# First batch's residual by a transposed DMA copy and VectorE adds, a new order of the first jobs, and two last stores on GpSimd's queue

## The chip, the cores and the metric

The kernel runs on one core of a Trainium2 chip. The metric is the device time of one execution in microseconds (us). A core has five engines with instruction streams of their own: TensorE (PE; its weight loads are listed as PEld), VectorE (DVE), ScalarE (ACT), GpSimd (POOL) and SyncE (SP). They meet through semaphores. SP, ACT and POOL also issue DMAs, which 16 DMA engines carry out. Matrix products land in PSUM, which the kernel uses as 8 banks of 128 x 512 fp32. Everything else lies in SBUF, 128 partitions wide.

## What is computed

Random-feature attention (8 batches, 8 heads, 576 tokens, 64 channels, 128 features), and an MLP mixer over its result, per batch 576 tokens x 512 channels:

```python
def phi(x):                      # x scaled by D ** -0.25
    h = x @ omega.T - (x * x).sum(-1, keepdims=True) / 2
    return exp(h - h.max(-1, keepdims=True)) / sqrt(m)
kv, z = phi(k).T @ v, phi(k).sum(tokens)
x = (phi(q) @ kv) / (phi(q) @ z + 1e-6)      # heads side by side: 576 x 512
u = x + (relu(x.T @ w_tok1) @ w_tok2).T      # token mix, 256 hidden
out = u + relu(u @ w_ch1) @ w_ch2            # channel mix, 1536 hidden
```

Inputs and outputs are fp32; inside, the products run in fp16.

## The kernel before

**Tiles.** Each batch has 512 main tokens (four tiles j of 128) and 64 tail tokens. Tails of two batches share 128 partitions, and all tails are channel-mixed at the end as a ninth "batch" c = 8.

**Stages of a batch.** `attention` makes the features kp and qp, per pair of heads (hp): a product on TensorE, an exponential on ScalarE (L499), for keys a maximum `km` and its reciprocal on VectorE (L652, L654), the scaled values `vs`, the kv product (L673, L680), its copy (L284), the numerator (L706) and the division (L715, L716). The tail tokens' keys go through L534 and `kt_max` (L573 to L576). `token_mix` has two hidden tiles (t1, L749), four output tiles (t2, L762), four VectorE adds that make u = x + h (`uadd`, L765), and on SP a DMA transpose u -> uT (`ut_dma`, L770), since the channel mix needs u with channels on partitions. `channel_mix` has twelve hidden tiles (c1, L938, four 128x512 products each, and a relu into r3) and then its output. For batches 1 to 8 that output is `channel_out_fast`: products of prepared sums (L888) and VectorE additions that read u and the bank (L877).

**Batch 0 is different.** `token_mix_first` makes uT straight from TensorE; u itself is never made. Its channel output is the plain one: for each of four tiles j, twelve products over the hidden tiles (L972) in three parts, and before the last of them four 128x128 products of uT with an identity (L970), which transpose u back into the PSUM bank and add it there as the residual. `out_copy` (L977, through L284) then copies the bank to o, twice on ACT (j = 0 and 2) and twice on DVE (j = 1 and 3), and a store (L982) issues from SP.

**Loads.** Batches 0 and 1 are loaded as they lie and transposed on TensorE. From batch 2 on, GpSimd's DMAs cast q and k to fp16 into a scratch in DRAM (`load_transposed`: k's tail L368, k's main part L362, q L357) and SP brings them back with DMA transposes (L378) as kT and qT. Those, and batch 2's above all, are spoken of below. Values come by GpSimd's DMAs too (L335, tails vt L349).

**What sets the order.** Every piece of work is a job with an engine and a cost, numbered as it is created. `run` (L136) executes the jobs in the order of a list written out by hand, `ORDER` (L22). So each engine issues its own jobs in that order, and a job that waits holds all later ones of its engine. A negative number in `ORDER` is a warm-up product of zeros on a bank. `SLOT` (L83) says which buffer of a ring each job takes (8 banks; three each of u, uT, kT, qT; two each of o and r3). `MOVED` (L93) and `BY` (L20) move single jobs between DVE, ACT, POOL and SP. A bank is given back by the job that reads it last, and the next user on TensorE waits for that reader.

**The last stores.** The tails' outputs leave in twelve small stores at the end of `channel_out_fast` (L911 to L919, issued at L917): six shapes, each once from SP and once from ACT. `need` names which quarter of the result they wait for.

Of the kernel before, what the change touches and what calls it, by code (L numbers as in the profile page):

```python
# [12 lines left out]
ALU = mybir.AluOpType  # L13
# [9 lines left out]
    6, 5, 0, 2, 3, 1, 4, 17, 15, 19, 7, 10, 13, -1, -2, -3, -4, -5, -6, -7, 49, 12, 40, 47, 8, 41, 43, 42, 48,  # L23
    23, 44, 50, -8, 45, 11, 108, 9, 123, 110, 51, 52, 22, 125, 46, -1, -4, 71, 124, 79, 14, 53, 72, 109, 32, 93,
    81, 57, 54, 95, 18, 55, 114, 58, 80, 30, 76, 67, 77, 20, 56, 74, -7, -7, -7, 96, 85, 73, 82, 75, 94, 97, -4,
    111, 68, 83, 99, 126, 112, 98, 21, -2, -2, 199, 78, 129, 86, -3, 63, 128, 84, 100, -8, 87, 201, 64, 88, 16,
    115, -6, -1, 101, 91, 89, 102, 235, 92, 200, 130, 103, 113, 65, 104, 237, 90, 59, 24, 236, 106, 66, 116,
    105, 27, 137, 117, 107, 25, 252, 127, 131, 60, 33, 253, 118, 120, 132, 141, 121, 26, 122, 133, 61, 142, 119,
    31, 135, 143, 138, 254, 136, 34, 249, 134, 238, 250, 145, 202, 240, 149, 251, 139, 144, 150, 35, 146, 151,
    62, 140, 332, 241, 239, 147, 329, 152, 203, 69, 221, 148, 255, 207, 224, 209, 153, 225, 154, 28, 70, 161,  # L30
    226, 256, 222, 159, 208, 223, 156, 162, 227, 157, 204, 210, 206, 177, 211, 155, 228, 169, 212, 213, 160,
    167, 333, 205, 173, 214, 257, 175, 242, 258, 178, 163, 158, 29, 176, 328, 261, 259, 164, 229, 174, 215, 165,
    230, 216, 262, 233, 243, 171, 244, 334, 166, 247, 36, 217, 172, 184, 327, 170, 168, 219, 189, 220, 234, 231,
    179, 232, 245, 180, 248, 331, 246, 190, 218, 181, 260, 191, 182, 263, 264, 266, 265, 194, 267, 183, 192,
    268, 330, 272, 269, 274, 273, 270, 275, 335, 271, 385, 337, 185, 336, 276, 387, 338, 343, 386, 371, 345,
    357, 391, 186, 339, 344, 358, 193, 373, 461, 195, 187, 359, 392, 37, 372, 346, 340, 374, 348, 462, 196, 377,
    375, 347, 277, 376, 197, 463, 360, 341, 388, 378, 363, 393, 362, 299, 394, 390, 283, 364, 379, 284, 289,
    380, 300, 278, 361, 291, 464, 342, 365, 38, 292, 287, 366, 389, 285, 288, 349, 383, 367, 286, 293, 465, 290,
    281, 294, 384, 350, 368, 369, 395, 295, 467, 396, 188, 397, 370, 198, 602, 381, 351, 297, 382, 598, 352,
    398, 355, 353, 298, 279, 356, 296, 603, 354, 282, 301, 468, 280, 39, 480, 399, 481, 303, 474, 466, 402, 304,  # L40
    302, 597, 305, 476, 400, 307, 403, 308, 311, 482, 401, 475, 309, 494, 310, 505, 496, 491, 306, 404, 507,
    312, 410, 495, 408, 411, 506, 315, 492, 405, 493, 409, 406, 316, 508, 469, 407, 519, 318, 521, 412, 470,
    471, 520, 522, 319, 510, 477, 313, 478, 511, 600, 523, 509, 317, 512, 323, 320, 599, 472, 321, 525, 473,
    435, 322, 526, 421, 497, 513, 422, 413, 524, 314, 479, 527, 498, 423, 436, 514, 325, 528, 414, 483, 601,
    415, 529, 499, 416, 530, 515, 427, 484, 500, 516, 531, 503, 731, 431, 428, 604, 532, 517, 417, 518, 736,
    501, 737, 419, 418, 502, 432, 733, 324, 485, 424, 433, 732, 486, 420, 504, 487, 425, 434, 488, 489, 429,
    426, 490, 630, 430, 533, 610, 534, 437, 612, 438, 611, 536, 441, 632, 442, 445, 535, 443, 537, 444, 631,
    439, 540, 446, 644, 655, 541, 544, 656, 542, 440, 646, 538, 326, 543, 449, 657, 545, 645, 539, 547, 450,
    546, 658, 627, 661, 660, 641, 452, 642, 628, 548, 629, 735, 447, 643, 659, 453, 613, 647, 605, 616, 607,
    457, 618, 734, 606, 614, 633, 648, 451, 617, 615, 608, 557, 634, 569, 609, 558, 619, 553, 649, 561, 554,  # L50
    620, 458, 565, 1006, 549, 566, 869, 650, 562, 635, 662, 559, 550, 636, 448, 570, 868, 637, 663, 560, 567,
    664, 454, 651, 667, 460, 738, 653, 555, 668, 654, 867, 563, 652, 621, 564, 639, 551, 622, 556, 640, 623,
    638, 625, 552, 665, 571, 666, 455, 626, 572, 624, 747, 573, 775, 748, 669, 574, 670, 568, 575, 749, 577,
    672, 777, 578, 776, 456, 581, 671, 579, 459, 673, 580, 871, 739, 750, 576, 741, 761, 674, 752, 582, 751,
    678, 675, 676, 740, 763, 679, 585, 762, 742, 680, 677, 587, 681, 586, 682, 789, 767, 764, 778, 588, 780,
    765, 766, 870, 768, 583, 589, 779, 790, 781, 743, 791, 593, 873, 590, 1003, 875, 792, 584, 877, 769, 1008,
    793, 591, 753, 794, 782, 876, 744, 594, 925, 872, 745, 697, 592, 754, 878, 691, 698, 1001, 927, 695, 770,
    874, 926, 795, 596, 687, 1002, 746, 755, 696, 783, 688, 773, 701, 774, 756, 796, 784, 759, 757, 699, 760,
    758, 771, 787, 700, 785, 692, 797, 689, 798, 772, 801, 705, 690, 802, 879, 786, 703, 706, 702, 799, 693,
    704, 788, 683, 800, 685, 684, 711, 694, 928, 686, 803, 911, 804, 707, 712, 806, 713, 805, 708, 715, 709,  # L60
    807, 710, 595, 714, 912, 810, 716, 930, 812, 929, 811, 814, 913, 808, 813, 719, 815, 809, 817, 720, 816,
    914, 818, 880, 883, 916, 722, 882, 881, 917, 1005, 721, 884, 915, 723, 885, 918, 886, 900, 724, 888, 897,
    727, 889, 1007, 899, 898, 725, 931, 890, 919, 819, 728, 920, 932, 887, 903, 730, 902, 891, 831, 1004, 901,
    892, 933, 726, 904, 825, 934, 832, 923, 833, 924, 1137, 841, 834, 893, 895, 842, 837, 894, 826, 820, 829,
    838, 921, 905, 823, 906, 896, 907, 937, 824, 835, 908, 909, 821, 836, 910, 922, 935, 839, 822, 938, 827,
    840, 936, 717, 828, 847, 830, 1017, 843, 1014, 939, 1019, 940, 848, 1018, 844, 1015, 942, 718, 1016, 849,
    851, 943, 845, 941, 729, 1034, 852, 1009, 1048, 1011, 944, 846, 1010, 1035, 948, 850, 946, 1049, 945, 950,
    1050, 947, 855, 1036, 949, 951, 1059, 1062, 856, 952, 1061, 1031, 857, 1023, 1032, 1064, 1060, 858, 1033,
    1138, 1065, 1063, 853, 859, 1066, 860, 1020, 1045, 1012, 1022, 863, 1046, 1021, 1037, 1013, 861, 1047, 854,
    1038, 973, 1051, 963, 1024, 953, 1052, 1067, 967, 1068, 964, 954, 1053, 1025, 974, 1054, 959, 862, 864,  # L70
    1069, 1071, 965, 1072, 866, 1139, 1026, 1057, 1039, 966, 1027, 971, 968, 1028, 865, 1055, 1029, 960, 972,
    961, 1040, 1070, 1041, 1043, 1030, 955, 1058, 969, 956, 1042, 957, 1056, 970, 962, 1044, 975, 958, 1073,
    977, 976, 1074, 978, 981, 1076, 982, 1075, 983, 985, 1077, 984, 979, 1078, 986, 1084, 980, 1080, 1079, 1087,
    1082, 1081, 989, 1085, 1088, 987, 990, 1140, 991, 1083, 1086, 992, 1145, 993, 994, 1147, 1146, 997, 995,
    1161, 1093, 1162, 1105, 1097, 1106, 998, 1103, 1111, 1104, 996, 1107, 1112, 1148, 1089, 1108, 1109, 1090,
    1098, 1101, 1110, 1095, 1094, 988, 1099, 1096, 999, 1091, 1100, 1102, 1153, 1117, 1092, 1118, 1000, 1163,
    1113, 1119, 1121, 1114, 1149, 1122, 1115, 1155, 1154, 1125, 1120, 1156, 1141, 1126, 1143, 1128, 1144, 1159,
    1129, 1142, 1127, 1151, 1130, 1116, 1133, 1152, 1150, 1131, 1134, 1136, 1157, 1164, 1165, 1160, 1132, 1123,
    1158, 1166, 1169, 1173, 1170, 1167, 1177, 1174, 1175, 1171, 1124, 1185, 1176, 1135, 1181, 1168, 1172, 1183,
    1182, 1179, 1178, 1184, 1187, 1180, 1201, 1190, 1188, 1189, 1202, 1186, 1191, 1197, 1192, 1204, 1195, 1198,  # L80
    1210, 1209, 1199, 1196, 1203, 1193, 1207, 1200, 1208, 1212, 1194, 1211, 1206, 1205,
]
SLOT = (  # L83
    "0010234056072110300612204735102705162011013422653131321705100372251101422307112015460726045331020410"
    "1506202741312504300161723463752131214023015013220136735207215100243726004310360721402263142010307312"
    "6003504115201051431722105643100171246710022430561270106332415101306132514322031125042111020036010231"
# [33 lines left out]
class Planner:  # L120
# [41 lines left out]
    def engine(self, usual):  # L162

        return MOVED.get(len(self.jobs), usual)
# [3 lines left out]
def kernel(  # L168
# [758 lines left out]
    def channel_mix(c, key, jt):  # L927
# [30 lines left out]
        if fast:  # L958
            channel_out_fast(c, key, jr)
            return  # L960
# [85 lines left out]
```

## Time and profile before

| what | value |
| --- | --- |
| time, median of 3 runs (lowest to highest) | 279.51 us (279.39 to 279.87) |
| the profiled execution: its time, its span | 279.96 us, 278.2 us |
| granted TensorE clock | 0.998 |
| 0 to 20 us: busy PE / DVE / ACT / POOL | 16.36 / 12.73 / 12.71 / 17.75 |
| 20 to 48 us | 28.00 / 22.02 / 18.13 / 18.57 |
| 48 to 57 us | 8.66 / 4.03 / 3.15 / 0.00 |
| 57 to 72 us | 14.63 / 12.81 / 12.54 / 7.62 |
| 72 to 85 us | 12.92 / 12.59 / 8.68 / 6.00 |
| 85 to 262 us | 177.00 / 146.22 / 80.60 / 42.60 |

The profile is of one execution. Its span runs from the first instruction to the last; the execution's time is that of the device around it. Busy times are of instructions that compute; DMA-issuing ones (SPq, ACTq, POOLq) are listed in the timeline but not counted. In a timeline row stand the start, the duration, the engine, the line of code, the operation, output <- inputs with their tiles, and in brackets how long the engine had been idle and what ended that. Rows of one line that follow each other are joined (x4). The chain that ended last is followed back from the last instruction, at each step to what released it.

### The profile page before, as it was taken

How to read it: one execution, taken by the hardware profiler on the slowest of the kernel's cores; microseconds unless marked ns; L12 is line 12 of the kernel's file. 1: busy time of each engine (PE TensorE's matmuls, PEld its weight loads, DVE VectorE, ACT ScalarE, POOL GpSimd, SP SyncE). 2: the span in 40 equal slices, each digit the busy share in tenths (PEclk: the TensorE clock that was granted, in tenths of full speed). 3: DMA queues.
4: the chain of work that ended last, by engine and by line, in shares of the span. 5: the costliest groups of instructions: out<-in, count | busy, mean ns of one | idle time of the engine just before them, and what ended most of it. 6: DMA issues, size and time to landing. Idle time of an engine off the chain costs nothing.

```text
span 278.2 us, 6130 instructions
## 1 busy us (share of the span) xinstructions
PE 268.6 (97%) x2459; PEld 167.2 (60%) x2459; DVE 220.2 (79%) x462; ACT 136.9 (49%) x284; POOL 92.5 (33%) x115
## 2 busy tenths in 40 slices
PE   7799999999999999999999999999999999999992
PEld 3458555444557655756676657655676477456781
DVE  3779678397996999987999799969995991595892
ACT  2788942397585337625756546635745500211200
POOL 8896782063722480076019600600052000000000
PEclk9999999999999999999999999999999999999999
DMA  7999999999996999979999987750342204030134
GB/s 192 173 201 197 206 209 157 183 211 170 202 204 136 188 180 179 189 138 156 202 182 191 236 104 113 179 123 0 103 71 84 88 10 87 0 153 0 75 105 125
DMA packets 84204, 39.66 MB, mean 143 GB/s; under 512 B 64208, under 2 KB 80784, under 8 KB 83984
## 3 DMA queue, kind: packets, MB, share of 16 engines
q0 software_dynamic: 34368, 17.48, 44.8%
q1 hardware_dynamic: 47504, 16.16, 29.2%
q10 hardware_dynamic: 2304, 5.64, 5.2%
q8 instruction: 19, 0.31, 0.4%
q14 instruction: 9, 0.07, 0.1%
HBM read 35.95 MB, written 16.52 MB: 189 GB/s over the span
## 4 chain that ended last, share of the span: by engine, by line
PE 75%; DMA 9%; DVE 6%; POOL 5%; issue 2%; ACT 1%; DVEq 0%; POOLq 0%; SPq 0%
PE bank L938 27%; PE bank L888 26%; PE bank L762 3%; PE bank L749 3%; DMA kT<-k 3%; PE bank L628 2%; PE bank L673 2%; DMA r<-in_q_dram 2%; DMA k<-in_k_dram 2%; PE bank L706 2%; PE bank L640 2%; DVE km L652 2%; POOL vs L293 2%; DMA vt<-in_v_dram 1%; DVE T L448 1%
## 5 line engine op out<-in xcount | busy, mean ns | idle before, releaser
L938 PE MATMUL bank<-uT,wc 128*128 128x512 f16 x376 | 89.5, 379 | 0.0
L288 ACT ACTIVATE r<-bank 128x512 f16<-128x512 f32 (+1 forms) x86 | 48.2, 600 | 78.9 <-PE bank L938 68.1
L293 POOL TENSOR_TENSOR vs<-v,vs 128x512 f16<-128x512 f16 x32 | 33.6, 1059 | 92.7 <-DVE vs L654 60.9
L938 PEld LDWEIGHTS <-wc 128*128 128x128 f16 x424 | 38.8, 98 | 37.3 <-issue 0.3
L888 PEld LDWEIGHTS <-r 128*128 128x128 f16 x384 | 36.9, 98 | 8.1 <-issue 0.7
L499 ACT ACTIVATE qp<-bank 128x512 f16<-128x512 f32 x64 | 36.7, 619 | 10.1 <-PE bank L640 7.3
L652 DVE TENSOR_REDUCE km<-kp 128x8 f16<-128x1024 f16 x32 | 38.7, 1208 | 2.6 <-ACT kp L499 2.4
L499 ACT ACTIVATE kp<-bank 128x512 f16<-128x512 f32 x64 | 35.7, 615 | 6.7 <-PE bank L628 5.5
L290 DVE TENSOR_SCALAR r<-bank 128x512 f16<-128x512 f32 (+1 forms) x40 | 26.1, 670 | 7.8 <-PE bank L938 6.8
L716 DVE TENSOR_TENSOR x<-bank,rc 128x320 f16<-128x320 f32 x62 | 30.5, 492 | 2.1
L888 PEld LDWEIGHTS <-S 128*128 128x128 f16 x288 | 28.0, 98 | 5.6 <-issue 0.4
L877 DVE TENSOR_TENSOR o<-u,bank 128x512 f32<-128x512 f16 x28 | 19.0, 679 | 7.8 <-PE bank L888 7.7
L888 PE MATMUL bank<-T,r 128*128 128x256 f16 x192 | 23.8, 273 | 0.0
L888 PE MATMUL bank<-T,S 128*128 128x256 f16 x192 | 23.6, 273 | 0.1
L888 PE MATMUL bank<-wc,r 128*128 128x256 f16 x192 | 23.4, 273 | 0.0
L765 DVE TENSOR_TENSOR u<-x,bank 128x512 f16<-128x512 f16 x28 | 17.7, 680 | 4.7 <-PE bank L762 4.7
L877 DVE TENSOR_TENSOR o<-o,bank 128x512 f32<-128x512 f32 (+1 forms) x27 | 16.5, 615 | 3.0 <-PE bank L888 2.6
L706 PEld LDWEIGHTS <-qp 128*128 128x128 f16 x256 | 13.8, 98 | 7.9 <-DVE kvsb L284 0.2
L715 DVE RECIPROCAL rc<-bank 128x5 f32<-128x5 f32 x62 | 11.5, 185 | 5.2 <-PE bank L708 3.9
L706 PE MATMUL bank<-kvsb,qp 128*128 128x65 f16 x256 | 15.5, 193 | 0.0
L673 PEld LDWEIGHTS <-kp 128*128 128x128 f16 x256 | 11.0, 98 | 5.5 <-issue 1.2
L762 PE MATMUL bank<-r,w 128*128 128x512 f16 x56 | 14.1, 381 | 0.0
(116 smaller groups left out, 364.9 us busy)
## 6 DMA issues: line engine op xcount, KB each, us to landing
out_dram<-o ACTq DMA_DIRECT2D x9, 512.0 KB, 3.2
q<-in_q_dram POOLq DMA_DIRECT2D x6, 576.0 KB, 9.2
wc<-in_moe_w_ch_dram POOLq DMA_DIRECT2D x4, 768.0 KB, 13.3
k<-in_k_dram POOLq DMA_DIRECT2D x6, 512.0 KB, 8.1
v<-in_v_dram POOLq DMA_DIRECT2D x6, 512.0 KB, 9.7
out_dram<-o SPq DMA_DIRECT2D x5, 512.0 KB, 3.3
r<-in_q_dram POOLq DMA_DIRECT2D x4, 256.0 KB, 7.9
v<-in_v_dram POOLq DMA_DIRECT2D x4, 256.0 KB, 8.2
```

The source lines that it names most:

```text
L288: nc.scalar.activation(out=out, in_=in_, func=AF.Relu)
L290: nc.vector.tensor_relu(out=out, in_=in_)
L293: (nc.gpsimd if eng == "POOL" else nc.vector).tensor_tensor(**kw)
L499: nc.scalar.activation(out=out, in_=in_, func=AF.Exp, bias=0.0, scale=1.0)
L652: nc.vector.reduce_max(out=mx, in_=kpv, axis=AX.X)
L706: nc.tensor.matmul(ps[:, k, j * 65 : (j + 1) * 65], st, s[:, i, 0 : D + 1], start=True, stop=True)
L716: nc.vector.tensor_tensor(out=t_x[place("x", b)][:, :, (2 * hp + hs[0]) * D : (2 * hp + hs[0] + n) * D].rearrange("p j (i d) -> p i j d", ...
L762: nc.tensor.matmul(ps, w2_of(tb, j), r1[:, tb, :], start=(tb == 0), stop=(tb == NT - 1))
L765: nc.vector.tensor_tensor(out=t_u[place("u", b)][:, j, :], in0=t_x[place("x", b)][:, j, :], in1=bank(n), op=ALU.add)
L877: nc.vector.tensor_tensor(out=o, in0=a, in1=ps, op=ALU.add)
L888: nc.tensor.matmul(ps[:, j * DH : (j + 1) * DH], a[:, cb, j * P : (j + 1) * P], w[:, cb, :], start=(bank_of(b, j0) not in held and j == j0 ...
L938: nc.tensor.matmul(ps, wc1[:, db, cb * P : (cb + 1) * P], moving(db), start=(db == 0), stop=(db == ND - 1))
```

## The change

Three things at once.

1. *Batch 0's residual.* The sixteen identity products leave TensorE. A new job `u_back` on SP transposes uT into a buffer of the u ring by DMA. The four copies from the bank become VectorE additions of u and bank, all on DVE, which wait for `u_back`.
2. *The order.* `ORDER`, `SLOT` and `MOVED` are new for the jobs of the first two batches, with a few swaps of neighbours later. The new job shifts all later numbers by one. `u_back` stands in SP's order right behind the back-transpose of batch 2's keys and ahead of that of its queries; uT of batch 1 follows. In GpSimd's order q's cast of batch 2 now stands ahead of the main part of k's. Warm-up products go from 20 to 25. Twelve jobs of ACT are on DVE after it (two of them the copies above), eleven of DVE on ACT, one of POOL on DVE, and two of batch 0's loads issue from ACT instead of SP.
3. *The last stores.* The two that need quarter "22" (128 KB each, one on SP and one on ACT before) issue from GpSimd.

In the file after, lines behind `ORDER` stand one later or one earlier than before: L378 is L379, `u_back` is L963, the additions are L977, the stores L981, the tail stores L918.

```diff
+        def u_back():
+            nc.sync.dma_start_transpose(out=t_u[place("u", c)].rearrange("p j (a c) -> p (j a) c", a=ND), in_=t_uT[place("uT", c)].rearrange("p j a c -> p (j a c)"))
+        j_u = dma("SP", key + 0.3, 2.6, u_back, deps=jt, take=[("u", c)], give=[("uT", c)], cost=3.5)
...
                     for cb in range(4 * part, 4 * part + 4):
-                        if cb == NCB - 1:
-                            for db in range(ND):
-                                nc.tensor.matmul(ps[:, db * P : (db + 1) * P], t_uT[place("uT", c)][:, j, db, :], ident16,
-                                                 start=False, stop=False, skip_group_check=True)
                         nc.tensor.matmul(ps, r3[:, cb, j * P : (j + 1) * P], wc2[:, cb, :], start=(cb == 0), stop=(cb == NCB - 1))
...
-            def out_copy(j=j, n=n, e_out=e_out):
-                copy(e_out, t_o[place("o", (c, j // 2))][:, j % 2], bank(n))
-            jo = add(e_out, 0.69, k2, out_copy, deps=[prev], take=[("o", (c, j // 2))], give=[("bank", n)])
+            def out_add(j=j, n=n):
+                nc.vector.tensor_tensor(out=t_o[place("o", (c, j // 2))][:, j % 2], in0=t_u[place("u", c)][:, j, :], in1=bank(n), op=ALU.add)
+            jo = add("DVE", 0.69, k2, out_add, deps=[prev, j_u], take=[("o", (c, j // 2))], give=[("bank", n), ("u", c)])
...
-                    eng = engine("ACT" if h else "SP")
+                    eng = engine("POOL" if need == "22" else "ACT" if h else "SP")
```

Of `ORDER`, the stretch around batch 2's back-transposes. Jobs before: 331 is kT and 330 qT of batch 2, 181, 186, 191, 196 are the last parts of the four output products, 182, 187, 192, 197 the copies. Jobs after: 332 is kT, 179 `u_back`, 331 qT, and 183, 188, 193, 198 are the additions.

```diff
-    179, 232, 245, 180, 248, 331, 246, 190, 218, 181, 260, 191, 182, 263, 264, 266, 265, 194, 267, 183, 192,
-    268, 330, 272, 269, 274, 273, 270, 275, 335, 271, 385, 337, 185, 336, 276, 387, 338, 343, 386, 371, 345,
+    246, 171, 158, 247, 173, 172, 164, 264, 265, 36, 195, 178, 266, 190, 180, 267, 332, 181, 268, 271, 191, 272,
+    174, 269, 179, 273, 275, 274, 196, 276, 192, 270, 331, 182, 336, 344, 338, 185, 346, 277, 337, 183, 358,
```

## The prediction

> **What bounds the kernel now.** I read the busy times first, then the 40 slices, then the chain that ended last. 0.2% of the time, 0.56 us, is about what a measurement of this kernel can tell from no change.
>
> ```profile
> PE 268.6 (97%) x2459; PEld 167.2 (60%) x2459; DVE 220.2 (79%) x462; ACT 136.9 (49%) x284; POOL 92.5 (33%) x115
> ...
> PE   7799999999999999999999999999999999999992
> ...
> PE 75%; DMA 9%; DVE 6%; POOL 5%; issue 2%; ACT 1%; DVEq 0%; POOLq 0%; SPq 0%
> ```
>
> TensorE is busy 97% of the span and is short of work only in the first slices and the last. By the windows it has all 177.00 of 177 us from 85 to 262, and the changed order leaves that stretch nearly as it was. So the time is decided by when TensorE leaves the first two batches, and by the tail behind its last matmul. The chain's longest pieces before 85 us lead to one place, batch 2's keys:
>
> ```profile
> 40.84 6.61 DMA k<-in_k_dram
> ...
> 47.54 8.19 DMA kT<-k
> ```
>
> Here are the queues around it: SyncE (SP), TensorE, VectorE (DVE), each from its timeline.
>
> ```profile
> 47.54 6.15 SPq L378 DMA_TRANSPOSE kT<-k  x1
> ...
> 54.35 2.61 SPq L378 DMA_TRANSPOSE qT<-q  x1
> 57.06 2.06 SPq L770 DMA_TRANSPOSE uT<-u  x1
> ```
>
> ```profile
> 49.00 0.39 PE L970 MATMUL bank<-ident,uT 128*128 128x128 f16 x4
> ...
> 55.77 0.28 PE L534 MATMUL bank<-omT,kT 64*128 64x128 f16 x4 [0.34 <-DMA kT<-k]
> ```
>
> ```profile
> 56.79 0.69 DVE L573 TENSOR_REDUCE kmt<-kpt 128x4 f16<-128x512 f16 x1
> ...
> 59.40 0.69 DVE L284 COPY o<-bank 128x512 f32<-128x512 f32 x1
> ...
> 66.07 0.30 DVE L284 CAST kvsb<-bank 128x130 f16<-128x130 f32 x1 [1.15 <-PE bank L680]
> ...
> 69.02 0.69 DVE L290 TENSOR_SCALAR r<-bank 128x512 f16<-128x512 f32 x1 [0.38 <-ACT kvsb L284]
> ```
>
> A start, a duration, and in brackets the idle time before it with its releaser. SP's first row is an issue that takes 6.15 us because the transpose's packets start only at 51.0, when the GpSimd queue's casts (v landed at 50.73) have drained; it lands at 55.73, and TensorE had waited 0.34 for it. VectorE from 56.79 on idles 1.15 + 0.38 only, until 71.64.
>
> **The change, part by part.**
>
> *Identity matmuls go.* Four groups of four 128x128 matmuls; sixteen in 0.89 to 0.90 us of starts (56 ns each): **-0.90** of TensorE. Two groups lie ahead of the kT gate at 55.77, where TensorE waits anyway, so -0.45 of it buys a longer wait.
>
> *u_back comes.* A transpose of 512 KB, in SP's order right behind kT of batch 2 and ahead of qT of batch 2. Its nearest rows are uT<-u, the same size and pattern: issue 2.06 us. From the end of issue to landing the rows give 2.04 (kT, 53.69 to 55.73), 2.11 (qT, 56.96 to 59.07) and 2.98 (uT, 59.11 to 62.09).
> When does kT land? In the new GpSimd order q's cast of batch 2 (576 KB) stands ahead of k's, so k reaches its scratch later than 47.45. But kT's packets did not start then: they started when the whole queue was empty. Its casts are the same, and walking GpSimd's new order by the old landings I find it empty at 50.3 to 50.8 instead of 51.0; I take 0.6 off, kT's issue end at 53.1 and its landing at 55.1. (Bounds 54.0 and 56.5: without the hole that its packets show from 52 to 53.5, or with the whole slip of k.) u_back, issued next, then ends its issue at 53.1 + 2.06 = 55.15 and lands at U = 57.2 by the first two rows, 58.1 by the third. I take **U = 57.2**, whose rows are the direct neighbours. Behind it qT ends its issue 2.61 later, at 57.76, and lands at 59.8; uT at 59.8 and 62.8. Two stores that stood between them now stand behind. Their first readers on TensorE stood at 60.16 and 63.84: covered by 0.4 and 1.0; what exceeds that cover would be a wait of TensorE.
>
> The Trainium skill (VectorE: DVE Perf Modes, "The three transpose paths" and its rules) speaks against this edit: a 128x128 transpose takes 390 ns on TensorE and 1309 ns through the DMA, and TensorE is to be used where PSUM will do. By that figure, as an estimate, sixteen blocks one by one would take 20.9 us, u_back would land near 76 and the body would be some 19 us longer. The rows disagree, and I give it no chance: the sixteen blocks of uT landed 3.02 us behind qT.
>
> *The adds.* Four VectorE adds (0.60 us start to start: the copy of 59.40, behind which the next starts at 60.01) replace two copies on VectorE and two on ScalarE: VectorE **+1.20**. The first add stands in VectorE's order behind the four uadds and ahead of kt_max (L573), its vbd and all four km of batch 2. So u_back's wait holds them all, and TensorE too: the second bank of the last kp pair is the one that this add frees. TensorE would reach it at about 56.9 and goes on at U + 0.7 = 57.9: a stall of 1.0.
> VectorE's sum: from 56.79 to 71.64 are 14.85 us, less the idle 1.53, so 13.32 of work, plus 1.20: 14.52. Started at U + 0.1 it ends at U + 14.62. The place that was at 71.64 is shifted by U - 57.0: at 57.2, **+0.2**. The two idle gaps are used up, and the shift is kept: VectorE is without a gap from 69.0 to 85.4, TensorE waits for its add at 82.54, and from 85 on all of TensorE is dense. TensorE's own path (gate 0.6 earlier, the two identity groups behind it -0.45, the stall +1.0) comes to -0.05: VectorE's ends last, and the two do not add. Body: +0.2, by the bounds of U (56.0 to 58.5) -1.0 to +1.5.
>
> *New order, moved engines, five more warm-ups.* Ahead of 20 us TensorE has 16.36 of 20 and waits for loads; warm-ups fill such holes, 0. About as many jobs go from ScalarE to VectorE as back, VectorE has 12.73 of the first 20 us and 22.02 of the next 28: room. Walking the new order through the loads I come to the first channel product within 0.5 of where it was. An earlier one is lost at the kT gate; a later one has 0.34 + 0.45 = 0.8 of cover there. I take 0; uncovered, +0.5 at most.
>
> *Tail.*
>
> ```profile
> 268.88 6.07 SPq L917 DMA_DIRECT2D out_dram<-o  x7
> ...
> 270.85 3.40 ACTq L917 DMA_DIRECT2D out_dram<-o  x5
> ...
> 273.03 0.42 DVE L877 TENSOR_TENSOR o<-o,bank 128x256 f32<-128x256 f32 x1 [0.23 <-PE bank L888]
> ```
>
> VectorE ends at 273.45, but SP issues its seventh store only at 274.47, behind its sixth (to 273.93) and 0.46 of wait for an older store's completion; it lands at 276.88, ScalarE's last at 276.70, and the span ends 1.3 later. With one store less in each, the last pair can issue near 273.5 and lands, by 2.2 (SP, 273.40 to 275.59) to 3.0 from issue (ScalarE, 273.68 to 276.70), at 275.7 to 276.5. GpSimd's two have their data by 271.7 to 272.0; the nearest row, GpSimd's vt load of 72.29, landed 4.25 after its start: 276.0 to 276.3. The last landing of 276.88 thus moves by -0.4 to -0.9; I take **-0.5**, near the late rows. None is gained if GpSimd's land 0.6 later than that row.
>
> *Sum.* +0.2 - 0.5 = -0.3 on the profiled execution's 279.96 (span 278.2), so 279.7. That execution stands 0.45 above the median of 279.51; against the median: 279.2, and **279.3** with the uncertain head leaning late.
>
> **Rivals.**
> *A, the forecast:* 279.3 (own range 278.7 to 280.0), chance 0.40.
> *B, u_back early.* kT shares the DMA engines with the casts instead of waiting for them, or the hole at 52 is missed. Against it: not one packet of kT before 51.0 with casts in flight. For it: a transpose into an idle queue, the uT of 85.50, landed 4.55 after its start, kT 8.19. kT at 54.0, U = 56.0: -1.0 - 0.5 gives 278.0 to **278.2**. Chance 0.30. The Trainium skill (DMA: Bandwidth & Descriptors, "SWDGE vs HWDGE vs iDMA") says that GpSimd's and SP's DMAs feed different queues inside each DMA engine, which takes them in turn; by that rule kT would move from its issue on, and this rival is the forecast. The trace shows no such turn before 51.0.
> *C, slower: u_back is the new gate.* On SP behind kT, whose k is now behind q on GpSimd's queue. Full slip: q's cast landed 2.86 behind v (50.73, 53.59), so k lands at 50.3, kT at 56.4, U = 58.5. VectorE's first add, kt_max, the km behind it and TensorE's bank all wait: +1.5 - 0.5 = +1.0, **280.5**. It decides from U = 58.1 on (1.06 above 57.0 eats the tail and 0.56). For it: the 2.98 row. Against: the queue's end, not k, held kT. Chance 0.22.
> *D, the tail gives nothing* (GpSimd's stores land last): 279.5 + 0.2 = **279.7**, chance 0.08.
>
> **Chances.** Faster by over 0.2% (below 278.95): B and a quarter of A, 0.40. Slower (above 280.07): C, with a little of A and D, 0.24. Within: 0.36. The range takes in B and C: 278.0 to 280.6.
>
> **What would show it.** No L970 groups; u_back's landing between 56.5 and 57.7, and VectorE's first add right behind it; kt_max and TensorE waiting there for the add; the last landing near 276.4 less the body's shift. I am wrong if u_back lands outside 56 to 58.5, if TensorE gets holes ahead of 48 us, or if the dense part from 85 on shifts by another amount than the add did.

## The result, and the profile after

The changed kernel takes 287.18 us (median of 6 runs, 284.89 to 290.96), the kernel before 279.25 (6 runs, 278.93 to 279.87): ratio 1.026, 95% interval 1.0231 to 1.0289, so 6.5 to 8.1 us slower. (The ratio leaves out the run of 290.96, in which TensorE's granted clock was lower, 0.986.) The forecast was 279.3, the range ended at 280.6. The profiled execution took 287.64, with a span of 285.9, 7.7 above that of before.

The busy line and the 40 slices of TensorE from the page after:

```profile
PE 273.2 (96%) x2448; PEld 168.4 (59%) x2448; DVE 224.8 (79%) x464; ACT 136.8 (48%) x283; POOL 92.5 (32%) x116
...
PE   6999999969899999999999999999999999999992
```

TensorE has 11 recorded products fewer (sixteen identity products less, five warm-ups more) and is nevertheless busy 4.6 us longer: the same products took longer somewhere. The slices from 85 us on are as full as before. Laying each TensorE job's start beside its start in the trace before shows where the time came from: the first channel product 35.44 instead of 30.42, the kT gate 60.52 instead of 55.77 (+4.74), from 85 to 275 us nearly every product +7.24 to +7.28 (a few swapped neighbours aside), the last products +7.98, the end of the span +7.69. So nearly all of it is there when the first two batches are done, and the gate is 4.7 late before `u_back` has made TensorE wait. Some 4.0 of these are TensorE's own: without its waits for kT it would have been there at 59.41, before at 55.43.

SP's, TensorE's and VectorE's timelines around the gate, after:

```profile
54.64 3.69 SPq L379 DMA_TRANSPOSE kT<-k  x1
58.43 2.17 SPq L963 DMA_TRANSPOSE u<-uT  x1
60.65 2.59 SPq L379 DMA_TRANSPOSE qT<-q  x1
63.33 2.67 SPq L771 DMA_TRANSPOSE uT<-u  x1
```

```profile
60.52 0.29 PE L535 MATMUL bank<-omT,kT 64*128 64x128 f16 x4 [1.11 <-DMA kT<-k]
...
63.99 0.38 PE L629 MATMUL bank<-omT,kT 64*128 64x128 f16 x7 [1.61 <-DVE o L977]
```

```profile
63.24 0.69 DVE L977 TENSOR_TENSOR o<-u,bank 128x512 f32<-128x512 f16 x1 [4.94 <-DMA u<-uT]
63.85 0.68 DVE L574 TENSOR_REDUCE kmt<-kpt 128x4 f16<-128x512 f16 x1
```

kT is issued at 54.64 (before 47.54) and lands at 60.47; `u_back` follows and lands at 63.15; the first addition starts 0.09 later, after VectorE has been idle 4.94 for it, kt_max right behind it; and TensorE waits 1.61 for the bank that the addition frees. These are the waits that the prediction named, at the places that it named, some six us later. The waits are not the origin, though: TensorE and kT were both late ahead of them. The DMA view of 18 to 28 us, before and then after, shows GpSimd's queue (q0) in that stretch:

```profile
q0 software_dynamic: 3149, 1.96, 127.3%
```

```profile
q0 software_dynamic: 3034, 1.25, 108.2%
```

(Packets, MB, share.) Before, the queue carried 1.96 MB in these 10 us, after only 1.25: the loads stood in GpSimd's order behind its vector work (L294 at 16.81 and 20.04), which waited for VectorE. Batch 2's casts follow: k's main part is issued at 42.58 instead of 29.66 and lands at 54.54 instead of 45.65, v at 57.89 instead of 50.73; q, which was moved ahead, at 52.08 instead of 53.59.

### The profile page after: what moved, and what is told of

Read it like the earlier page. It is cut to its first block, busy times and chain, and to the rows that moved or that the text cites. A ratio compares the mean times of both kernels' runs of the same rounds, so it can differ in the third digit from the quotient of the medians.

```text
span 285.9 us, 6132 instructions
## 1 busy us (share of the span) xinstructions
PE 273.2 (96%) x2448; PEld 168.4 (59%) x2448; DVE 224.8 (79%) x464; ACT 136.8 (48%) x283; POOL 92.5 (32%) x116
## 4 chain that ended last, share of the span: by engine, by line
PE 75%; DVE 9%; DMA 8%; issue 2%; SPq 2%; ACT 2%; POOL 1%; DVEq 0%
PE bank L939 26%; PE bank L889 26%; DMA k<-in_k_dram 4%; PE bank L763 3%; PE bank L750 3%; PE bank L629 3%; DVE km L653 2%; PE bank L641 2%; PE bank L707 2%; PE bank L674 2%; DMA wc<-in_k_dram 2%; PE bank L473 2%; DMA u<-uT 2%; PE bank L1012 2%; SPq L379 1%
## 5 line engine op out<-in xcount | busy, mean ns | idle before, releaser
L294 POOL TENSOR_TENSOR vs<-v,vs 128x512 f16<-128x512 f16 x31 | 32.6, 1057 | 95.9 <-DVE vs L655 64.9
L500 ACT ACTIVATE kp<-bank 128x512 f16<-128x512 f32 x64 | 36.3, 612 | 17.8 <-PE bank L629 17.8
L291 DVE TENSOR_SCALAR r<-bank 128x512 f16<-128x512 f32 (+1 forms) x41 | 26.9, 671 | 8.1 <-PE bank L939 7.4
L918 POOL DMA_DIRECT2D out_dram<-o x2 | 1.3, 644 | 61.5 <-DVE o L878 61.5
L716 DVE RECIPROCAL rc<-bank 128x5 f32<-128x5 f32 x62 | 11.5, 185 | 5.4 <-PE bank L709 4.9
L629 PE MATMUL bank<-omT,kT 64*128 64x128 f16 x256 | 13.6, 228 | 1.7 <-DVE o L977 1.6
```

The source lines that it names most:

```text
L291: nc.vector.tensor_relu(out=out, in_=in_)
L294: (nc.gpsimd if eng == "POOL" else nc.vector).tensor_tensor(**kw)
L500: nc.scalar.activation(out=out, in_=in_, func=AF.Exp, bias=0.0, scale=1.0)
L629: nc.tensor.matmul(ps[e][:, c : c + M], m[half[e], r, :], omT[half[e]], start=True, stop=True)
```

## The experiments

These are the seventeen kernels, each timed beside the kernel before on the same chip. A diff of the order shows the part of the list that was edited. The numbers of a job differ by the presence of `u_back`: e2, e4, e8 and e15, which have it, use those of the kernel after (there `u_back`, of batch 0, is 179), all others those of before. A negative number is a warm-up.

| kernel | ratio to before (95%) |
| --- | --- |
| changed | 1.026 (1.0231 to 1.0289) |
| e1 order only | 1.0178 (1.0151 to 1.0205) |
| e2 residual only, behind kT | 1.022 (1.0202 to 1.0238) |
| e3 stores only | 0.9994 (0.9984 to 1.0003) |
| e4 changed, u_back ahead of kT | 1.0327 (1.028 to 1.0374) |
| e5 order, sixteen warm-ups out | 1.0217 (1.0187 to 1.0247) |
| e6 order, loads first | 1.0162 (1.0145 to 1.018) |
| e7 both | 1.022 (1.0193 to 1.0247) |
| e8 residual only, ahead of kT | 1.0311 (1.0263 to 1.0359) |
| e9 order, first product first | 1.0217 (1.0171 to 1.0263) |
| e10 new head, old rest | 1.0129 (1.01 to 1.0158) |
| e11 old head, new rest | 1.0421 (1.0384 to 1.0457) |
| e12 order, three more warm-ups | 1.0108 (1.0082 to 1.0134) |
| e13 e12, loads and product first | 1.0147 (1.0127 to 1.0168) |
| e14 before, three fewer warm-ups | 1.0019 (1.0005 to 1.0033) |
| e15 before, and the transfer alone | 1.0221 (1.0197 to 1.0244) |
| e16 e12, thirteen warm-ups out | 1.0148 (1.0124 to 1.0172) |
| e17 e12, seven out | 1.0138 (1.0086 to 1.019) |

Theory 1 after the result: the new order makes the head late, and `u_back` adds to it. Theory 2: the wait for `u_back` is the cost. The first four take the change apart.

**e1, the order alone.** The old residual and stores in the changed kernel:

```diff
-        j_u = dma("SP", key + 0.3, 2.6, u_back, ...)
+                                nc.tensor.matmul(ps[:, db * P : (db + 1) * P], t_uT[...], ident16, ...)
-                    eng = engine("POOL" if need == "22" else "ACT" if h else "SP")
+                    eng = engine("ACT" if h else "SP")
```

> This is the changed kernel with the old residual (sixteen identity products, four copies, all on VectorE) and the old stores: the new order alone. Theory 1 (the new order makes the head late: it empties GpSimd's queue of casts late, so kT of batch 2 lands near 60.5 instead of 55.73, and u_back only adds its own 2.5 behind it): kT of batch 2 lands at 60 to 61, time 4.5 to 5.5 above before, 283.8 to 284.8. Theory 2 (the order is neutral, the wait for u_back costs the time): kT at 55 to 56, time within 1 of before. Theory 3 (each part costs about a third): about 2.5 above before.

283.71 against 278.88: 1.0178, some 5.0 of the 7.3 us. kT landed at 59.60. Theory 1 holds for the order.

**e2, the residual alone**, in the order of before, `u_back` behind kT:

```diff
-    ... 331, 246,
+    ... 332, 179, 247,
```

> The kernel before with u_back and the VectorE additions alone, in its own old order and stores; u_back stands behind kT of batch 2 on SP. Theory 1: kT lands at 55.7 as before, u_back some 2.7 later at 58.4, and by the rule of the prediction (u_back's landing less 57.0) TensorE is 1.4 later from 85 us on: 280.4 to 281.0. Theory 2: the wait for u_back makes most of the loss, 284 or more. Rival to both: the 0.9 of TensorE that goes is kept, 278.4 to 279.0.

1.022, 6.1 us: far over theory 1's 1.4 although `u_back` landed at 56.33, 2.43 behind kT. TensorE's waits in e2, the longest first (total, times, longest):

```profile
PE bank L760 <- DVE o L974: 3.5, 1, 3.5
```

In the old order the four output tiles are finished between 49 and 62 us and their banks copied out at once; now a tile that is finished earlier holds its bank until `u_back` lands, and batch 1's token mix (L760) waits for a bank 3.5 us. And the wait costs twice. The windows of e2 (busy PE ... POOL, then the granted clock, DMA share, GB/s):

```profile
54.00:56.00 2.00, 0.00 (x0) 0.00 (x0) 0.00 (x0) 0.00 (x0) 0.00 (x0) 1.00 0.97 183
...
60.00:62.00 2.00, 2.00 (x18) 0.89 (x18) 1.93 (x5) 0.71 (x3) 0.78 (x1) 0.50 1.03 221
62.00:64.00 2.00, 2.00 (x19) 0.98 (x15) 0.45 (x2) 2.00 (x5) 1.98 (x4) 0.50 1.07 204
64.00:66.00 2.00, 2.00 (x10) 0.65 (x10) 1.39 (x2) 1.04 (x3) 2.00 (x3) 0.71 1.18 147
66.00:68.00 2.00, 2.00 (x16) 0.61 (x14) 1.90 (x4) 1.82 (x4) 0.27 (x2) 1.00 0.88 164
```

After the gap TensorE is granted half its clock (0.58 from 58, 0.50, 0.50, 0.71) for 6.8 us by the trace's clock records (58.34 to 65.16), and does half the work: about 3.4 us more. The Trainium skill (TensorE: Matmul & The Clock Gate, Part 1) says that an idle window of about 3.4 us puts TensorE to half rate and that it takes at least one busy window to release it. The gap of 3.5 agrees with the first; the release took 6.8 us here and in e8, and 3.4 in e4 and e15. In the changed kernel's profile, where the gaps were 1.11 and 1.61, the clock stayed at 1.00.

**e3, the stores alone.**

```diff
-                    eng = engine("ACT" if h else "SP")
+                    eng = engine("POOL" if need == "22" else "ACT" if h else "SP")
```

> The kernel before with the two stores on GpSimd's queue alone. In the changed kernel the last landing came 3.28 behind the last VectorE instruction, before 3.43, and the end 4.44 behind it, before 4.73: 0.15 to 0.3 faster, 278.9 to 279.1. The prediction's size was 0.5 faster, 278.75. Rival: GpSimd's stores land last, 0.2 or more slower.

0.9994: 0.2 faster to no change (+0.08 to -0.45 us). The 0.5 of the prediction was too much. GpSimd's two landed at 273.63 and 274.64, ahead of the last one, from ScalarE, at 276.09.

**e4, the changed kernel with `u_back` ahead of kT.**

```diff
-    ..., 152, ..., 332, ..., 179, ...
+    ..., 152, 179, ..., 332, ...
```

> The changed kernel with one job moved: u_back ahead of kT of batch 2 in SP's order, right behind the job that finishes uT (SP is idle there until kT). Theory 1: u_back lands before 45, kT still near 60.5; what u_back added behind the gate (7.27 late from 85 us on, 4.74 late at the gate) goes: 2 to 3 below the changed kernel, 284.2 to 285.2. Theory 2: most of the loss goes, 279 to 281. Rival: the additions were not what VectorE was late for, nothing changes, 286.5 to 287.5.

1.0327, worse than the changed kernel, against both theories and the rival. `u_back` was in flight from 34.04 to 50.24, kT landed at 62.06, TensorE waited 3.9 for it and fell to 0.50 from 62 to 64.

**e8, the same in the old order.**

```diff
+    ..., 148, 179, ...
-    ..., 332, 179, ...
+    ..., 332, ...
```

> The kernel before with u_back and the additions, u_back right behind the job that finishes uT, some 15 us ahead of kT, in the old order. In the changed kernel with u_back first it was in flight from 34.04 to 50.24 beside GpSimd's casts, and k's cast landed 1.35 later than without that. So: u_back lands near 46 to 48, the wait of 3.5 on TensorE and the slow clock behind it are gone, kT lands 0 to 1.5 later, the 0.9 of identity products goes: 278.0 to 280.0. Rival (a transpose among the casts costs as much as it moves, 512 KB at about 190 GB/s is 2.7 us): 281 to 282.

1.0311, against the expectation and its rival. kT landed at 59.20 instead of 55.73, TensorE waited 4.1, the clock fell to 0.50. Hidden time on an idle queue (SP had nothing to do there) was no hidden time for the DMA engines, as e15 shows.

**e15, the transfer alone**: before, complete, and besides it `u_back`, read by nobody.

```diff
+        j_u = dma("SP", key + 0.3, 2.6, u_back, deps=jt, take=[("u", c)], give=[("uT", c), ("u", c)], cost=3.5)
...
+    ..., 148, 179, ...
```

> The kernel before, complete with identity products and copies, and besides them the transposed copy of uT into u, behind the job that finishes uT, read by nobody: the price of the transfer by itself. With the additions in it (287.6) k's cast of batch 2 landed at 49.48 instead of 45.65 and kT at 59.20 instead of 55.73, TensorE waited 4.1 and then ran at half rate for some 6 us. Theory D (the DMA engines are full up to the gate, so 512 KB more come on top): the same, 285.5 to 288. Theory A (the additions' waits were it): 279 to 280.

1.0221, 6.2 us: theory D, the transfer itself is the cost, with nobody waiting for it, because it shares the DMA engines with the casts. SP's timeline, the queues of 37 to 45 us, and TensorE's longest wait in e15:

```profile
29.94 8.26 SPq L960 DMA_TRANSPOSE u<-uT  x1
50.59 6.40 SPq L376 DMA_TRANSPOSE kT<-k  x1
```

```profile
q0 software_dynamic: 1285, 1.25, 92.7%
q1 hardware_dynamic: 1283, 0.33, 30.6%
```

```profile
PE bank L532 <- DMA kT<-k: 4.0, 1, 4.0
```

Two queues have work, and in eight us 1285 packets of the one and 1283 of the other are carried: they take turns, packet by packet. A packet of the transpose is 0.33 MB / 1283 = 0.26 KB, of a cast 0.97 KB. So 512 KB of transpose are about 2000 turns, last 20.1 us from issue to landing (30 to 50), and their time is taken from the casts that lead to kT, which lands at 59.05. The Trainium skill (DMA: Bandwidth & Descriptors, "Queues, rings and completion order") says that each DMA engine goes round the queues that have work, packet by packet; this trace agrees to two packets in 1285.

How dear was it? k's cast landed 3.1 us later than before (48.72 for 45.65). At the 197 GB/s that the view gives for this stretch 512 KB are 2.7 us, so the casts lost about what the transfer moved, the size that e8's rival had. The rest of the 6.2 us comes behind the gate: TensorE's wait of 4.0 brought 3.4 us of half clock with it, and in this profile TensorE also waited 1.8 for uT. e8 is 2.5 us slower still; what its additions cost there was not tried.

The other runs look for what makes the new order's head late; all have the old residual and stores, as e1.

**e5, fewer warm-ups, e6, loads first, e7, both.** e5 drops all warm-ups behind the ninth; e6 moves the DMA issues of batch 1's q, wc1, wc2, w1m and batch 2's k main cast ahead of GpSimd's vector work (e6's edit, GpSimd's jobs alone):

```diff
-    ... 75, ..., 27, ..., 115, 30, 86, 18, 32, 130, 25, 31, 333, 24, 29, 21, 26, 33, 332, 203, 28, 34, 35 ...
+    ... 75, ..., 27, 30, 18, 32, 21, 115, 86, 25, 24, 26, 130, 29, 33, 31, 34, 35, 333, 332, 329, 203, 28 ...
```

> The new order alone (old residual, old stores; 283.7 before this run) with nine of its 25 warm-up products: the sixteen that stand behind the first nine are out. Theory W (the thirteen of them between 15.06 and 19.09 stand in TensorE's way and cost their 3.1 us): the products behind them start 2 to 3 earlier, 281 to 282, if GpSimd's queue follows; where only the gate of batch 2's kT is left, 283.0. Theory P (GpSimd's order is what makes the gate late) and the prediction's zero (they fill holes): 283.4 to 284.0.

> The new order alone with GpSimd's DMA issues moved ahead of GpSimd's vector work that waits for VectorE: the loads of batch 1's q, of wc1 and wc2 and the cast of batch 2's k stand as early as in the order before. Theory P (the queue ran dry from 17 to 28 us because the issues stood behind that work, 242, 333, 148, 279 and 219 KB per 2 us where before had some 380): it stays full, kT of batch 2 lands at 55 to 57, time 280.0 to 281.5 unless TensorE's own head is as late as the gate. Theory H (TensorE's head is late by itself, it waited only 0.5 for the gate): kT early, but time 283.0 to 283.7.

> Both edits on the new order alone: sixteen warm-ups out and GpSimd's issues first. If both theories hold half (TensorE's head and the gate are late by about the same, so each alone hides the other's gain): 279.5 to 281, clearly below each alone. If P alone holds: as the run with the loads first. If the cause is elsewhere (order of TensorE's jobs, the first loads): above 282.5.

e6 did what it should: q0 stayed full (1.99 MB from 18 to 28 us), kT landed at 55.30, earlier than before. And the time is 1.0162, as e1 (1.0178) within the intervals. The first reader of kT on TensorE, in e6:

```profile
58.60 0.29 PE L533 MATMUL bank<-omT,kT 64*128 64x128 f16 x4
```

At 58.60 and with no wait: theory H, TensorE comes late by itself, the dry queue was not the bound. e6 changes one thing more: it issues k's cast ahead of q's, where the changed kernel has q first. GpSimd's timelines, after and then e6:

```profile
42.03 0.56 POOL L358 DMA_DIRECT2D q<-in_q_dram  x1
42.58 0.57 POOL L363 DMA_DIRECT2D k<-in_k_dram  x1
```

```profile
31.84 0.56 POOL L361 DMA_DIRECT2D k<-in_k_dram  x1 [2.60 <-DMA wc<-in_moe_w_ch_dram]
...
40.86 0.56 POOL L356 DMA_DIRECT2D q<-in_q_dram  x1
```

So the early kT is the work of both; the time did not follow either of them. e5 and e7 did not come out faster, and e7 is 1.6 us above e6: with sixteen warm-ups fewer the clock fell to half again (e7: from 18.2 to 25.1 us).

**e9, e10, e11.** e9 puts the first key product ahead of the third group of key transposes; e10 runs the new order's first 110 entries and then the old order; e11 the old order's first 120 and then the new.

```diff
-    ... 41, 49, 8, 47, 50, 9, 17, 45, 48, 14, 42, 46, 10, -6, -7, 108, 43, ...
+    ... 41, 42, 49, 8, 47, 50, 9, 17, 48, 108, 45, 14, 46, 10, -8, -1, 43, ...
```

> The new order alone, with its first key product (and the two VectorE copies that it needs) ahead of the third group of key transposes and of two warm-ups, which moved behind it to other banks. Theory H1 (ScalarE is what TensorE waits for up to 40 us; in the new order its first exponential starts at 9.84 instead of 7.59 us, and that is carried through): the first exponential starts near 8.3, 1.3 to 1.6 earlier, and the time falls by 1 to 1.6, to 282.2 to 282.8 (283.7 before). Theory H2 (the order behind 20 us is the cause): 283.4 to 284.0.

> The new order up to its 110th entry (TensorE at 20.2 us, all loads and warm-ups up to there), then the jobs that are left in the old order; old residual, old stores. In TensorE's ledger (time that is not useful products) the new order stands 1.0 to 1.6 above the old one at 20 us and 3.3 to 3.8 at 40 us. Theory H1 (the late start of ScalarE is carried through, the rest only shows it): most of the 4.8 stays, 282 to 283.8. Theory H2 (what follows 20 us is the cause): 280 to 281.

> The reverse: the old order up to its 120th entry (TensorE at 19.8 us), then the jobs that are left in the new order without its further warm-ups; old residual, old stores. Theory H1: 279.0 to 280.5. Theory H2: 282 to 284.

e9: the first exponential started at 8.37 instead of 9.84, but the next group of them came at 12.29 (12.76 in the changed kernel) and ScalarE idled 2.15 in between; nothing was gained. Theory H1 in this form (the late first product makes the head late) falls. e10: 1.0129, 3.6 of 5.0 us (2.8 to 4.4) come with what stands ahead of 20 us. e11 is inconclusive: the mixture had a wait of its own (TensorE 4.4 and 6.6 us for loads that the second order issues too late for the first).

**e12, three more warm-ups, and e14, three fewer in the old order.** The head's products, TensorE's timeline of before, after and e12:

```profile
4.40 1.06 PE L472 MATMUL bank<-S,wc 128*128 128x128 f32 x8
5.57 0.66 PE L472 MATMUL bank<-S,wc 128*128 128x128 f32 x4
```

```profile
4.92 1.94 PE L473 MATMUL bank<-S,wc 128*128 128x128 f32 x8 [1.16 <-DMA wc<-in_k_dram]
7.29 1.11 PE L473 MATMUL bank<-S,wc 128*128 128x128 f32 x4 [0.43 <-DMA wc<-in_k_dram]
```

```profile
4.83 1.14 PE L471 MATMUL bank<-S,wc 128*128 128x128 f32 x8
7.25 0.66 PE L471 MATMUL bank<-S,wc 128*128 128x128 f32 x4 [1.28 <-DMA wc<-in_k_dram]
```

The same eight products take 1.06 before and 1.94 after. The new order has five warm-ups and then a hole of 1.16, the old one seven without a hole. The clock column gives 1.00 in both stretches, but it counts time without a clock record as full. The kept traces' first record, to full clock, stands at 4.07 us before, at 13.41 after and at 5.02 in e12, and the durations change there: ahead of it the products run at half rate.

```diff
-    ... -1, -2, -3, -4, -5, 41, 49, ...
+    ... -1, -2, -3, -4, -5, 41, -6, -7, -8, 49, ...
```

> The new order alone with three more warm-up products in the hole of 1.2 us behind the first five (TensorE waits there for the first keys, 3.5 to 4.9 us). Theory C (in the new order that hole keeps TensorE at half rate up to 13.3 us: the same group of four key transposes takes 1.11 us against 0.66, eight key products 0.54 against 0.33, while the order before had seven warm-ups in a row and is at full rate from 4.4 us): the groups behind 5 us take 0.66 and 0.33, the head is 1 to 2 earlier at 20 us, time 281.5 to 282.7 (283.7 without). Theory L (the first loads decide when the head runs): rate up, time 283.3 to 284.0.

```diff
-    ... 13, -1, -2, -3, -4, -5, -6, -7, 49, ...
+    ... 13, -1, -2, -3, -4, 49, ...
```

> The kernel before with four instead of seven warm-up products at its start; nothing else. Theory C: the hole ahead of the first transposes holds TensorE at half rate for some us, the head loses 1 to 3, 280.2 to 282.2. Otherwise (they only fill a hole, the prediction's zero): 278.9 to 279.4.

e12 has the full rate from 5 us and 1.0108: 2.0 of the order's 5.0 us come back, with three products added. e14, whose first record stands at 8.08, loses 0.5 (0.1 to 0.9), less than expected: in its profile TensorE reaches the gate of batch 2's kT at 55.35, no later than before. Theory C, the cold rate, holds for two fifths of the order's loss.

**e13, e16, e17.** e13 adds e6's and e9's edits to e12; e16 takes the thirteen warm-ups at 12.61 and 15.12 us out of e12, e17 the first seven (shown).

```diff
-    ... 115, 112, -7, -7, -7, -7, -8, -8, -1, 53, ...
+    ... 115, 112, 53, ...
```

> The new order alone with the three warm-ups, the first key product first, and GpSimd's loads first. If the head's loss is the sum of cold clock, late first product and late loads, each hidden by the next: 279.5 to 281.5. If it lies in the order in which queries and keys of batch 0 come to ScalarE (idle 3.4 us longer up to 15 us): 282.5 to 283.7.

> The new order alone with the three early warm-ups (3.4 above before) and without the thirteen at 12.61 and 15.12 us. The first seven of these stand ahead of query transposes whose load landed at 12.35, the other six ahead of a query product. Theory W (at full rate they are in TensorE's way for up to 3.1 us): ScalarE gets its queries 1.5 to 3 earlier, 1 to 2.5 less, 0.9 to 2.4 above before. Theory Z (what stands behind them waits for copies and banks anyway): within 0.4 of the run with them, 3.0 to 3.8 above. Rival: the holes bring the half rate back, 5 or more above.

> The same with only the first seven out. Theory W: half of that gain, 0.6 to 1.5 less than with them, 1.9 to 2.8 above before; theory Z: 3.0 to 3.8 above.

None gained on e12. In e16 the granted clock was 0.88 up to 20 us and 0.75 to 24, in e17 0.91: whatever the warm-ups cost by standing ahead of the queries, they earned by keeping the rate. What makes the remaining 3.0 us of the new order stays open. If the 2.0 of the cold rate are part of e10's 3.6, about half of the 3.0 is set ahead of 20 us; neither GpSimd's loads, nor the first product, nor fewer warm-ups gave it back. e12 reaches the gate 1.6 us later than before and waits for nothing there; up to that place its eight warm-ups more than before take 1.65 us of TensorE. ScalarE, behind its first instruction and up to 15 us, is idle 8.4 us in the changed kernel and 6.2 in e12, against 4.7 before, but no run took that idle time away.

## Why the prediction was wrong

*The head.* "Walking the new order through the loads I come to the first channel product within 0.5 of where it was": it came 5.0 late (35.44 for 30.42). This is the step that failed. The term was put at 0, +0.5 at most, and e1 sizes it: 5.0 us. The prediction names no rate for the head, and the rate was half up to 13.4 us (11.5 in e1); e12 shows 2.0 of the 5.0 to come from that, and the cause of the other 3.0 stays open. Up to the gate both kernels do the same products, warm-ups and identity products aside. From start to start TensorE spends there 1.9 us more on the sixteen fp32 key transposes, 1.6 more on the key features, 1.0 on the five further warm-ups and 0.7 more idle; 0.6 less on the query features and 0.45 less on identity products. The cover of 0.8 at the gate was far too small for that.

*Warm-ups at 0.* Wrong in kind: they set the rate of what follows. Three more gave 2.0 back (e12), sixteen fewer took 1.6 us (e7 against e6).

*kT at 55.1.* It landed at 60.47. "I find it empty at 50.3 to 50.8": the queue was empty at 57.9, since its loads were issued late. Yet e6 shows that this was not the bound. The reading that kT's packets "started when the whole queue was empty" was wrong too: in the trace before the first came at 51.15, while q's cast landed only at 53.59, and e15's transpose shared the engines with the casts for 16 us. Behind its issue kT's first packet came 1.3 us (the changed kernel) to 4.2 us (e15) later. One thing holds in all nineteen traces: kT landed 1.8 to 3.4 us behind the last of batch 2's main casts, whichever that was, q in the old order (53.59, then 55.73) and v in the new one (57.89, then 60.47). The walk took v for the last one in the old order as well. Why kT follows the last cast is not shown.

*u_back at kT + 2.1.* It took 2.68 (60.47 to 63.15); in e2 2.43. Right in kind. The rule "U - 57.0" gives 6.15 for U = 63.15, the body was 7.27.

*What that wait is worth.* The forecast for `u_back` and the additions was +0.2. On top of the order's 1.0178 they make about 2.3 us of the changed kernel's 1.026. Alone, in the old order, they cost 6.1, and the order alone 5.0, together 7.3: the two do not add. Both make TensorE late around the same gate, which fits, but no run takes the overlap apart. The prediction had counted no gap long enough to lower the clock; in e2 and e8 the half clock cost about 3.4 us beside waits of 3.5 and 4.1, in e4 about 1.7 beside 3.9.

*Identity products, -0.90.* They went, and nothing of it could be seen in the time, as forecast.

*Tail, -0.5.* Mis-sized: alone 0.2 (e3), and no gain at all lies within the interval. In the changed kernel's profile one VectorE addition of the tail also waited 0.97 for a store of the ring to land.

*Rivals.* C ended on the right side, by the mechanism of `u_back` behind a late kT and with U beyond its 58.1; but its 280.5 was 6.7 too low, and its reason, k's cast behind q's, was never tried alone: e6 puts k ahead of q and fills the queue as well, and kT landed at 55.30. B's sharing of the engines is what the DMA engines do (e15), and it works against the kernel: the casts pay for it. The Trainium skill's rule of different queues taken in turn (DMA: Bandwidth & Descriptors, "SWDGE vs HWDGE vs iDMA"), which I set aside because no packet came before 51.0, was right about the sharing: e15's packets show it. That kT would move from its issue on, which the prediction drew from the rule, no run shows.

## What to carry to other kernels

A new order of the first microseconds has to be walked with the rate that TensorE will have there: look at the durations of its first products, holes and warm-ups included, and take a gap of over three us in mid-kernel at one and a half times to twice its length, as e4, e2 and e8 had it. A transfer on an idle queue is not hidden while the DMA engines are full: a transpose takes turns with the casts beside it, so price it by what those lose (3.1 us for 512 KB in e15), at the gate that they feed. And before trusting that a dry queue is the bound, fill it, as e6 did.

## What the runs showed that was not expected

TensorE's rate has two levels, and the clock column shows only some of it. Behind gaps of 3.5 to 4.1 us it shows 0.50, for 3.4 or 6.8 us. A head at half rate it shows as 1.00, because the records begin only with the first step to full clock (13.41 us in the changed kernel). And a long gap is not needed: in e7, e16 and e17 the clock fell to half for 3.4 or 6.8 us with no gap of TensorE above 1.3 us behind the first product, while in the changed kernel it stayed up behind one of 1.61; no run shows where the line lies.

One execution of e5 took 553.57 us: its profile has the 128x512 products of L937 at 679 ns each instead of 379, from the first to the last, and not one clock record, which the column gives as 1.0. One of e7, without a profile, took 700.93. The other executions of these two kernels took 284.8 to 295.7, and why those two were so long stays open.
